# A list scheduler gets ten more rounds with shaken keys: the order of the attention stage in a gated linear attention and mixture-of-experts kernel

## The chip, the cores and the metric

The kernel runs on one core of a Trainium2 chip. The metric is device time in microseconds (us); lower is better. The core has five engines that run side by side, each through its own instructions in their order: TensorE (PE in the profile, its weight loads PEld), VectorE (DVE), ScalarE (ACT), GpSimd (POOL) and SyncE (SP), which here only issues transfers (DMA). An instruction that needs another engine's result waits for it, and everything behind it on its own engine waits too. So the order in which each engine's instructions stand decides how long the engines wait for each other.

## The reference

Two blocks follow each other: a gated linear attention and a mixture of experts with one expert per token. With B = 4, H = 8, S = 768 positions, D = 48 per head, N = 3072 tokens of 384 values, 8 experts with 1024 hidden values:

```python
mag = np.sqrt(a_re * a_re + a_im * a_im)
scale = np.minimum(mag, 0.999) / (mag + 1e-06)
a_re_n, a_im_n = (a_re * scale, a_im * scale)
for t in range(S):
    ar, ai = (a_re_n[:, :, t, :, None], a_im_n[:, :, t, :, None])
    new_re = ar * S_re - ai * S_im
    new_im = ar * S_im + ai * S_re
    kv = np.einsum('bhd,bhe->bhde', k[:, :, t], v[:, :, t])
    S_re, S_im = (new_re + kv, new_im)
    y[:, :, t] = np.einsum('bhd,bhde->bhe', q[:, :, t], S_re)
...
x = np.ascontiguousarray(attn_out.transpose(0, 2, 1, 3)).reshape(B * S, H * D)
...
logits = x @ w_gate
expert_idx = np.argmax(logits, axis=1)
...
for e in range(E):
    mask = expert_idx == e
    xe = x[mask]
    h = np.maximum(xe @ w1[e], 0.0)
    ye = h @ w2[e]
    out[mask] = gate_w[mask, None] * ye
```

`gate_w` is the softmax weight of the chosen expert. The change alters no arithmetic: both kernels compute all of this.

## The kernel before

The attention's recurrence is done in chunks of 128 positions: cumulative products of the complex gates (X), queries multiplied with them and keys divided by them, then products of matrices on TensorE. The expert part follows.

What matters here is that the attention part, the routing and the first two tiles of the first expert aren't emitted in the order in which the code stands. Each piece of work becomes an `Op` with an engine, the time in which it keeps that engine busy, a `late` time after which its result can be used, and what it needs. The times are the author's constants:

```python
        def dve(cols, emit, after=(), free=(), first=5):
            return op("V", cols / 960 + 0.068, cols / 960 + 0.19, emit, after, free, first)

        def act(cols, emit, after=(), free=(), first=5, n=1):
            return op("A", n * 0.08 + cols / 1200, n * 0.08 + cols / 1200 + 0.15, emit, after, free, first)

        def pe(passes, emit, after=(), free=(), first=5):
            return op("T", passes * 0.111, passes * 0.111 + 0.45, emit, after, free, first)

        def dma(late, emit, after=(), free=()):
            return op("S", 0.62, late + 1.0, emit, after, free)
```

`after` holds operations whose result it reads, `free` those that must be done before it may overwrite a buffer. `turns` walks through time: whenever an engine is free, it takes the able operation with the smallest key.

```python
def turns(ops, needs, users, ready, key, begin):
    ...
    for _ in ops:
        t, e = min((max(clock.get(e, 0.0), min(x[0] for x in l)), e) for e, l in able.items() if l)
        x = min((x for x in able[e] if x[0] <= t), key=lambda x: key[x[1]])
        able[e].remove(x)
        clock[e] = begin(x[1], t, clock.get(e, 0.0))
        ...
```

`in_time` does this ten times. The first round's key is the longest way to the end. After each round the schedule is run backward from the end, and the latest starts found there become the keys of the next round. The round whose schedule ends first, by those constants, is kept.

```python
def in_time(ops):
    ...
    key = {o: (o.first, -way[o]) for o in ops}
    best = None
    for _ in range(10):
        start, slow, twice = {}, [0.0], set()
        ...                                   # TensorE counts double for a while after an idle time
        turns(ops, needs, users, lambda o: ..., key, begin)
        end = max(start[o] + o.late for o in ops)
        if best is None or end < best[0]:
            best = end, sorted(ops, key=lambda o: start[o]), start

        back = {}
        ...
        turns(ops, users, needs, lambda o: ..., {o: -start[o] - o.busy for o in ops}, begin_back)
        key = {o: -back[o] - o.busy for o in ops}
    return best[1]
```

At the end the operations are emitted in the kept order: `for o in in_time(ops): o.emit()`. Each engine then runs its own in that order.

The steps of one tile (two and two thirds heads of one batch) that are spoken of below: `fold` sums squares on VectorE (`fs`), takes Ln and Exp on ScalarE (`fl`), corrects that value by a Newton step on VectorE and multiplies queries and keys into packs, which transfers move to `QX` and `KX`, one buffer per head:

```python
                o = dve(n, lambda: vtt(s, f2[:, 0], f2[:, 1], ALU.add), [sq], old["fs"])
            ...
            ln = act(n, lambda: A.activation(l, s2, func=ACT.Ln, bias=w_bias[:, 1:2]), [o], old["fl"])
            ex = act(n, lambda: A.activation(l, l, func=ACT.Exp, scale=-1.0), [ln])
            prod = [dve(n, lambda u=u: vtt(q_to[u], pu[u], by_chunk(qs[:, :, at]), ALU.mult), there + [lq], free[0]) for u in range(2)]
            ...
            o = dve(n, lambda: vtt(s, s2, l, ALU.mult), [ex], [g] + old["fs"])
            ...
            o = dve(n, lambda: vstt(l, s, -2.0, l, ALU.add, ALU.mult), [o])
            o = dve(n, lambda: vtt(l, l, ks[:, :, at], ALU.mult), [o, lk])
            kprod = [dve(n, lambda u=u: vtt(k_to[u], pu[u], by_chunk(l), ALU.mult), [o], free[1]) for u in range(2)]
```

`front` builds the products X; between blocks it carries a state on (`carry`, `zc`), which reads `last`, copied by ScalarE. `attention` runs per chunk and pair of heads: a score matmul from KX and QX into a PSUM bank, a masking product on VectorE (`ak<-bank,causal`), a copy on ScalarE, the output matmuls, their copy `ys`, a transpose of the state, its copy `st` (read by the next chunk's outputs), and a matmul that mixes the heads into rows `xf`. `send` routes finished rows and moves them to `sorted_x`; `early` computes the first two tiles of the first expert. Then come all experts, which are written in plain order and aren't in the list.

## Time and profile before

| | before |
|---|---|
| time, median of 3 runs | 665.49 us (665.45 to 667.85) |
| span of the profiled execution | 662.9 us |
| TensorE busy | 547.0 us (83%), mean granted clock 0.932 |
| VectorE busy | 368.9 us (56%) |
| ScalarE busy | 289.4 us (44%) |
| GpSimd busy | 79.0 us (12%) |
| moved by transfers | 89.81 MB, 135 GB/s |

The shares of the whole span mix two parts. The page also gives the busy time in forty slices of the span, where they come apart, and the trace answers for any stretch. A busy TensorE is not TensorE at its peak, since matmuls are pipelined and their ends are modelled. A wait is put down to the operation that came last before it ended.

### The profile page before, as it was taken

Reading aid. Unit: us, or ns where it says so; the run is one execution under the profiler, and the core shown is the slowest. Engines: PE = TensorE matmul, PEld = TensorE weight load, DVE = VectorE, ACT = ScalarE, POOL = GpSimd, SP = SyncE. Lnnn points to the kernel's source line nnn. Section 1 sums busy time; section 2 is a strip of 40 time slices with the busy share of each in tenths; the row PEclk is TensorE's granted clock in tenths of the full one; section 3 lists DMA queues with packets and bytes.
Section 4 is the critical chain, followed back from the end, with each engine's and each line's share of the span. In section 5 each row is a group of like instructions: output and inputs, shape, how many; then the busy total and the mean of one; then the engine's idle time right before and its main releaser. Section 6 shows DMA issues by size and latency. Waiting matters only on the chain. (4 is left out here: it accounts for less than half of the span.)

```text
span 662.9 us, 8204 instructions
## 1 busy us (share of the span) xinstructions
PE 547.0 (83%) x2594; PEld 334.5 (50%) x2594; DVE 368.9 (56%) x782; ACT 289.4 (44%) x940; POOL 79.0 (12%) x96
## 2 busy tenths in 40 slices
PE   1541288968899478968998999999999999999993
PEld 0220145636565345645566675555555555655552
DVE  5999999999999999999735121111111202010100
ACT  6555488788998788866743101010111100010100
POOL 9100000000004004003003110111101020101111
PEclk9865599998999689988999999999999999999997
DMA  9694866277624766178479434444554440100000
GB/s 260 144 244 118 194 166 160 80 191 174 177 72 130 188 158 177 52 172 203 107 275 400 89 130 124 139 141 138 151 139 135 117 124 32 36 6 24 9 12 29
DMA packets 77635, 89.81 MB, mean 135 GB/s; under 512 B 25341, under 2 KB 67343, under 8 KB 75536
## 3 DMA queue, kind: packets, MB, share of 16 engines
q1 hardware_dynamic: 74000, 79.33, 44.3%
q0 software_dynamic: 3584, 9.87, 4.2%
q8 instruction: 22, 0.36, 0.2%
q14 instruction: 29, 0.24, 0.1%
HBM read 54.31 MB, written 16.63 MB: 107 GB/s over the span
## 5 line engine op out<-in xcount | busy, mean ns | idle before, releaser
L136 PE MATMUL bank<-xt,big 128*128 128x448 f32 (+1 forms) x384 | 136.1, 514 | 1.1 <-DVE xt L888 1.1
L136 PE MATMUL bank<-big,ht 128*128 128x384 f32 (+1 forms) x608 | 136.8, 420 | 0.0
L136 PE MATMUL bank<-QX,KX 128*128 128x224 f32 (+1 forms) x384 | 94.4, 378 | 35.0 <-DMA KX<-pk 26.1
L136 PEld LDWEIGHTS bank<-big,ht 128*128 128x128 f32 (+1 forms) x608 | 84.5, 168 | 53.6 <-issue 7.0
L136 PEld LDWEIGHTS bank<-xt,big 128*128 128x128 f32 x384 | 71.1, 190 | 63.3 <-issue 60.8
L136 PEld LDWEIGHTS bank<-QX,KX 128*128 128x128 f32 x384 | 68.5, 205 | 51.1 <-issue 34.7
L136 ACT ACTIVATE big<-big 128x576 f32<-128x576 f32 (+3 forms) x77 | 68.6, 903 | 16.4 <-DVE big L136 15.1
L909 DVE TENSOR_SCALAR ht<-bank 128x448 f32<-128x448 f32 (+1 forms) x32 | 18.9, 591 | 101.9 <-PE bank L136 101.9
L136 ACT ACTIVATE QX<-diag,KX 96x48 f32<-96x48 f32 x280 | 72.5, 335 | 1.9 <-DMA KX<-pk 1.7
L911 ACT ACTIVATE ht<-bank 128x448 f32<-128x448 f32 (+1 forms) x32 | 16.6, 517 | 121.8 <-PE bank L136 121.8
L136 PE MATMUL two<-big,ident 128*128 128x512 f32 (+1 forms) x112 | 43.2, 542 | 29.8 <-ACT big L136 25.8
L788 POOL DMA_INDIRECT sorted_x<-xf,slot x24 | 29.8, 1242 | 316.0 <-DVE big L136 155.3
L136 PE MATMUL bank<-ak,vb 128*48 128x224 f32 (+1 forms) x384 | 54.1, 365 | 15.2 <-ACT ak L136 12.9
L136 DVE TENSOR_TENSOR big<-big,big 128x576 f32<-128x576 f32 (+3 forms) x86 | 65.0, 766 | 0.9 <-ACT big L136 0.2
L922 ACT ACTIVATE yo<-bank,gt 128x384 f32<-128x384 f32 x15 | 8.7, 581 | 122.4 <-PE bank L136 122.4
L136 DVE TENSOR_TENSOR big<-big 128x288 f32<-128x288 f32 (+5 forms) x108 | 55.2, 518 | 6.2 <-ACT big L136 5.4
L269 POOL DMA_INDIRECT out_dram<-yo,to x22 | 21.4, 972 | 230.1 <-ACT yo L922 184.9
L136 DVE TENSOR_TENSOR ak<-bank,causal 128x256 f32<-128x256 f32 x96 | 39.9, 417 | 15.3 <-PE bank L136 15.0
L136 PEld LDWEIGHTS two<-big,ident 128*128 128x128 f32 x112 | 22.9, 240 | 49.8 <-issue 32.9
L136 PE MATMUL bank<-QX,st 128*48 128x224 f32 (+1 forms) x320 | 43.3, 350 | 0.8 <-ACT st L136 0.8
L136 PE MATMUL bank<-across,ys 128*128 128x104 f32 x192 | 37.7, 287 | 5.3 <-ACT st L136 2.4
L136 ACT ACTIVATE ys<-bank 128x224 f32<-128x224 f32 (+1 forms) x96 | 32.3, 342 | 16.0 <-PE bank L136 15.6
(126 smaller groups left out, 555.5 us busy)
## 6 DMA issues: line engine op xcount, KB each, us to landing
big<-in_moe_w_dram SPq DMA_DIRECT2D x16, 1536.0 KB, 9.1
KX<-pk SPq DMA_DIRECT2D x44, 146.2 KB, 4.3
QX<-pk SPq DMA_DIRECT2D x44, 144.0 KB, 3.5
sorted_x<-xf SPq DMA_DIRECT2D x8, 731.5 KB, 6.2
xq<-sorted_x SPq DMA_DIRECT2D x28, 168.0 KB, 8.6
big<-in_a_re_dram SPq DMA_DIRECT2D x16, 288.0 KB, 4.6
big<-in_a_im_dram SPq DMA_DIRECT2D x16, 288.0 KB, 4.5
qt<-in_q_dram SPq DMA_DIRECT2D x12, 384.0 KB, 3.9
```

The lines of the kernel that those rows point to most:

```text
L136: return lambda *a, **kw: self.tc.keep_in_program_order(f(*a, **kw))
L269: move = nc.gpsimd.indirect_dma_start(out=rows, out_offset=bass.IndirectOffsetOnAxis(ap=index, axis=0), in_=y, in_offset=None, bounds_chec ...
L788: move = nc.gpsimd.indirect_dma_start(out=sorted_x[:, :], out_offset=bass.IndirectOffsetOnAxis(ap=slot[:, i:i + 1], axis=0), in_=xfs[(b * ...
L909: nc.vector.tensor_scalar_max(ht[:, f, cols], h, 0.0)
L911: nc.scalar.activation(ht[:, f, cols], h, func=ACT.Relu)
L922: nc.scalar.activation(y, o, func=ACT.Copy, scale=gt[:, i, 0:1])
```

## The change

The scheduler gets twenty rounds in place of ten. The first ten are as before. From the eleventh on, every key gets a random shift before the round: up to 4 us either way in the eleventh, 0.6 times as much in each further round (2.4, 1.44, ..., 0.04 us). The shifts come from a small generator of numbers with a fixed first value, so that the build always gives the same order. The best round of all twenty is kept, again by the author's constants. The purpose is to leave an order on which the forward and backward passes have settled, and to try others near it.

```diff
+SHAKE = 2004214
 ...
 def in_time(ops):
+    bits = SHAKE * 2862933555777941757 + 3037000493
+
+    def shake(width):
+        nonlocal bits
+        bits = (bits * 6364136223846793005 + 1442695040888963407) % (1 << 64)
+        return ((bits >> 33) / (1 << 30) - 1) * width
+    for _ in range(4):
+        shake(0)
     needs = {o: list(dict.fromkeys(o.after + o.free)) for o in ops}
 ...
     key = {o: (o.first, -way[o]) for o in ops}
     best = None
-    for _ in range(10):
+    for turn in range(20):
+        if turn >= 10:
+            key = {o: key[o] + shake(4 * 0.6 ** (turn - 10)) for o in ops}
         start, slow, twice = {}, [0.0], set()
```

The kept order before comes from the fifth round; the kept order after comes from the seventeenth, the seventh of the new ones.

## The prediction

> **What bounds the kernel now.** I read the views from coarse to fine: the slices of the page, the table of stretches, then the waits and the order in time of VectorE.

> First the slices of the page, each digit a fortieth of the span (16.6 us), in tenths of busy time:

> ```profile
> PE   1541288968899478968998999999999999999993
> DVE  5999999999999999999735121111111202010100
> ACT  6555488788998788866743101010111100010100
> ```

> VectorE stands at 9 from the second slice to the nineteenth, then TensorE at 9 to the end. So there are two regimes, one after the other. I took the seams from the order of instructions in time and asked for the busy time of each stretch. Columns: from and to, length, then busy us and count for PE, PEld, DVE, ACT, POOL, and the granted clock, DMA share and GB/s.

> ```profile
> 6.20:20.00 13.80, 4.50 (x8) 2.27 (x8) 10.35 (x15) 10.58 (x17) 13.13 (x20) 1.00 0.80 228
> 20.00:324.15 304.15, 220.84 (x1294) 141.80 (x1295) 297.05 (x584) 232.78 (x800) 23.97 (x18) 0.87 0.60 156
> 324.15:353.95 29.80, 27.39 (x206) 19.12 (x207) 12.22 (x40) 13.55 (x56) 0.00 (x0) 1.00 0.73 264
> 353.95:379.69 25.74, 23.01 (x98) 15.85 (x97) 7.39 (x45) 4.01 (x17) 6.81 (x7) 1.00 0.68 217
> 379.69:652.95 273.26, 271.22 (x993) 155.42 (x991) 39.04 (x82) 25.85 (x48) 29.31 (x31) 1.00 0.31 90
> ```

> The reader is to see four things. From 20 to 324 us VectorE works 297.05 of 304.15 us: **7.1 us of idle time are all that an order can take from it directly**. From 324 to 380 us TensorE works 50.4 of 55.5 us: first the rest of attention, then the two early tiles of the first expert. From 380 us the experts keep TensorE at 271.2 of 273.3 us. And 10 us of end follow. The experts are not in the list that the change reorders.

> Who holds VectorE in those 304 us is in its waits (total, times, longest):

> ```profile
> DVE fs L136 <- ACT fl L136: 2.2, 3, 1.2
> DVE zc L136 <- ACT last L136: 1.2, 2, 0.7
> DVE big L136 <- ACT big L136: 0.5, 2, 0.4
> DVE free_row L136 <- ACT big L136: 0.2, 1, 0.2
> ```

> That is 4.1 us in 8 waits, all for ScalarE, none for a DMA or a matmul. The other 3.0 us lie in gaps too short to be listed. Six lines of VectorE's order in time (start, busy us) show what these are:

> ```profile
> 316.69 0.55 DVE L136 TENSOR_TENSOR pk<-big,qt 128x384 f32<-128x384 f32 x1
> 317.16 0.41 DVE L136 TENSOR_TENSOR ak<-bank,causal 128x256 f32<-128x256 f32 x1
> ...
> 318.23 0.54 DVE L136 SCALAR_TENSOR_TENSOR fl<-fs,fl 128x384 f32<-128x384 f32 x1
> 318.81 0.56 DVE L136 TENSOR_TENSOR fl<-fl,kt_in 128x384 f32<-128x384 f32 x1
> 319.40 1.03 DVE L136 TENSOR_TENSOR pk<-big,fl 128x384 f32<-128x384 f32 x2
> ...
> 323.34 0.56 DVE L136 TENSOR_TENSOR fs<-fs,fl 128x384 f32<-128x384 f32 x1 [1.22 <-ACT fl L136]
> ```

> Where the next operation doesn't read the one before it, it starts ahead of that one's recorded end: 317.16 against 316.69 + 0.55 = 317.24, so 0.08 early. Where it does read it, it starts after: 318.81 against 318.77, 319.40 against 319.37. Over the whole stretch I took the medians: 67 such pairs at +0.034 us, the other neighbours at -0.082 us. **A dependent pair side by side costs 0.116 us more** than the same two with something else between them. The last line is the longest of the eight waits.

> [...] The trace shows 0.50 in the slice from 60 to 80 us, after a wait of 26.1 us for the first KX; nothing in the change removes that wait, as shown below.

> **The change part by part.** No instruction is added or removed on the chip: the ten extra rounds are work of the build. Both orders hold the same 675 operations on VectorE, 710 on ScalarE, 435 on TensorE, 268 transfers on SyncE and 26 on GpSimd. So busy sums stay, and only waits can change. I compared the two built orders, engine by engine and place by place.

> 1. What stays. VectorE's order is the same for its first 70 operations, TensorE's for its first 5, ScalarE's for its first 45. The start (6 us before the first product, the idle time to 20 us) and the half clock before 80 us therefore stay. The round that won is the seventh of the ten new ones, with 490 of VectorE's 675 operations in other places, by 3 places on average.

> 2. What lies ahead of the end. I added up VectorE's durations from the trace ahead of the last product into KX (the last head's keys): 307.4 us of work in both orders, a difference of 0.0. For the first head of the second batch it is 4.2 us later, for the second tile of the last batch 1.0 us earlier. So the new order puts no less work in front of the critical product; VectorE can reach it sooner only by idling less.

> 3. Dependent pairs. Up to that product the old order has 71 neighbours in which the second reads the first, the new one 58. 13 x 0.116 us = 1.5 us less.

> 4. The eight waits. A product `fs<-fs,fl` waits for Ln and Exp on ScalarE; what hides them is the VectorE work between the sum of squares and that product. Old and new, in us of such work: 2.15 and 4.29 at the product that now waits 0.77 us (at 84.7 us), 2.12 and 3.48 at the one that waits 0.11 (132.2 us), 0.82 and 1.47 at the one that waits 1.22 (the last line above). Of the 13 products nine get more cover, two of them (227.5 and 317.5 us) 0.3 to 0.4 us less, the rest about the same. For `zc<-last,carry`, which waits for two copies on ScalarE: 0.63 and 1.90 at 117.1 us, 1.18 and 1.10 at 199.9 us (waits 0.51 now), 1.26 and 0.65 at 305.5 us (waits 0.67 now), so one may get worse. I count 0.8 + 0.1 + 0.6 us saved and 0.2 us lost, so **4.1 us of named waits become about 2.8**, and 0.2 for smaller ones: 1.5 us less. ScalarE's own queue was moved too, by 6 places on average, and that I can't add up; it makes this term the loosest.

> 5. The tail. TensorE idles 5.1 us between 324 and 380 us, in waits of at most 0.9 us for ScalarE and VectorE on a chain that goes back and forth (outputs, their copy, transpose, its copy, next outputs). The new order keeps that chain; the last chunk's scores stand at places 376 and 377 of 435 in place of 377 and 379. The transfers change more: the last six loads of KX are issued only from 329.4 us now, behind four loads of sorted rows and three of QX, though their products end at 326.5 us. In the new order four QX loads go ahead of the first KX, in time in which SyncE waits anyway. TensorE has other work at that point, so I count 0 for the tail, with 1 us either way.

> Sum: -1.5 - 1.5 + 0 = **-3.0 us**. TensorE idles 2 to 7 us in most stretches of 20 us between 80 and 324 us, so an earlier VectorE should pull it along, and the experts, 273.3 us, follow unchanged. 665.5 - 3.0 = 662.5 us.

> **The rivals.** *VectorE was never the limit that matters; the chain on TensorE is.* For it: from 324 us on TensorE is full, and if its work before that is held by copies on ScalarE (15.2 us in 15 waits for `ak` alone), VectorE's gain ends as a longer wait. Against it: TensorE idles throughout. It would give 665 us. *ScalarE takes over.* It works 19.8 of 20 us from 160 to 180 us and 19.7 in the next 20, so a VectorE that is 3 us ahead there meets a full queue, and operations that the shaking put in front of a needed Exp would cost VectorE new waits. It would give 665 to 668 us. *Transfers.* SyncE issues in one queue, each issue some 0.6 us; one moved behind a late source blocks all behind it. The eleven loads of the tail were reordered, so a loss of 1 to 3 us there is possible: 664 to 667 us.

> **Range and chances.** The dependent pairs are counted, so that term is firm to half a us; the waits may end anywhere from -3 to +2 us; the tail within 1.5 us. Together some 3 us either way: 659.7 to 665.8 us. The 7.1 us of idle time in the first regime and the 5.1 us in the tail cap a gain at 12.2 us, under 2% of 665.5 (13.3 us), so faster by over 2% is nearly out of reach; a loss of that size would need one transfer or wait gone badly wrong.

> **What would show it.** In the changed profile: the stretch from 20 us to the last `fs<-fs,fl` near 321 us in place of 323.3, with VectorE idle near 5 us in it; named waits of VectorE near 2.8 us, still for ScalarE; the first matmul of the experts near 376.7 in place of 379.69 us; the experts at 273 us. Wrong I would be if VectorE's waits rose or named a DMA or a matmul, if its lead were there at 320 us and gone at 377, or if the experts' stretch itself moved.

## The result, and the profile after

The changed kernel takes 672.25 us (median of 4 runs, 670.41 to 672.66) against 666.12 us before in the same session: **ratio 1.0083, 95% interval 1.0054 to 1.0111**, so 0.8% slower. Run once more beside other kernels it took 672.91 us, ratio 1.0101 (1.0076 to 1.0127). The prediction was 662.5 us, at most 665.8: wrong in sign. By the scheduler's own constants the kept order ends 3.6 us earlier than the old one (373.03 against 376.64 us); on the chip it ends 6 to 7 us later. Most single executions of one kernel lie within 3 us of their median, so a ratio counts here only with its interval.

The profiled execution has a span of 668.6 us (662.9 before). First the slices of the page:

```profile
PE   1551278967979587978898999999999999999993
DVE  5999999999999999899934102102111202010110
ACT  6555498877997778767843110010000010010100
```

VectorE's row of nines is broken once, in the slice from 267 to 284 us, and lasts one slice longer than before (the twentieth is a 9). Then the stretches, with seams at the same instructions as before (columns: from and to, length, busy us and count of PE, PEld, DVE, ACT, POOL, then granted clock, DMA share, GB/s):

```profile
20.00:330.82 310.82, 222.25 (x1295) 143.08 (x1295) 296.88 (x583) 233.41 (x800) 23.16 (x18) 0.86 0.61 153
330.82:360.85 30.03, 27.62 (x211) 19.32 (x211) 12.69 (x45) 14.05 (x60) 1.68 (x2) 1.00 0.76 277
360.85:385.35 24.50, 22.72 (x92) 15.31 (x91) 7.51 (x40) 3.59 (x13) 5.12 (x6) 1.00 0.67 208
385.35:658.90 273.55, 271.23 (x993) 155.42 (x991) 39.25 (x82) 25.85 (x48) 29.53 (x31) 1.00 0.31 90
```

The whole loss stands in the first line. It is 6.7 us longer than before (310.82 against 304.15), with the same VectorE work (296.88 against 297.05): VectorE idles 13.9 us instead of 7.1. The tail (30.03 + 24.50 = 54.5 us, against 55.5) is 1.0 us shorter, the experts are 0.3 us longer. The first expert matmul starts at 385.35 us (379.69 before). Who holds VectorE in the first stretch (total, times, longest):

```profile
DVE zc L148 <- ACT last L148: 2.0, 1, 2.0
DVE fs L148 <- ACT fl L148: 1.7, 3, 0.9
DVE free_row L148 <- ACT QX L148: 1.6, 1, 1.6
DVE big L148 <- ACT big L148: 1.6, 3, 1.1
DVE fs L148 <- ACT big L148: 1.4, 1, 1.4
DVE big L148 <- ACT xf L148: 0.8, 1, 0.8
...
```

All lines together are 11.1 us in 15 waits, against 4.1 in 8 before; 9.8 us of them name ScalarE, 1.3 us a matmul. `fs<-fs,fl`, the wait that I had worked on, did shrink (1.7 after 2.2; the 1.22 us before the last product is gone). What is new are single waits of 1 to 2 us at places where the old order had none: for `last`, for a `QX` copy, for products into `big`. The largest is at 273.77 us. This is ScalarE, then TensorE, in order of time just before it (start, busy us; in brackets idle time before, and what ended it):

```profile
264.54 0.68 ACT L148 ACTIVATE big<-big 128x576 f32<-128x576 f32 x1 [1.02 <-issue]
266.44 0.36 ACT L148 ACTIVATE ys<-bank 128x224 f32<-128x224 f32 x1 [1.22 <-remote]
...
269.22 0.27 ACT L148 ACTIVATE st<-bank 96x128 f32<-96x128 f32 x1 [1.76 <-PE bank L148]
...
273.21 0.34 ACT L148 COPY last<-big 128x192 f32<-128x192 f32 x1
273.45 0.29 ACT L148 ACTIVATE last<-big 128x96 f32<-128x96 f32 x1
```

```profile
264.00 0.55 PE L148 MATMUL bank<-QX,st 128*48 128x224 f32 x4
266.85 0.31 PE L148 MATMUL bank<-ident,ys 128*96 128x128 f32 x1 [2.30 <-issue]
```

The copies into `last` wait for nothing themselves: they stand in ScalarE's queue behind `ys` and `st` copies that came late and the QX products behind those. And `ys` at 266.44 us is odd. It reads a matmul whose record ends at 264.55 us, everything else it needs is older, yet it starts 1.9 us after that end and 1.2 us after the engine was free. In a second profile of the same kernel these are 4.1 and 3.45 us. In the profile of the kernel before, no operation that waits for TensorE has such an unexplained gap of over 0.5 us.

### The profile page after: what moved, and what is told of

It is laid out like the page before. It is cut to its first block, busy times and chain, and to the rows that moved or that the text cites. A ratio compares the mean times of both kernels' runs of the same rounds, so it can differ in the third digit from the quotient of the medians.

```text
span 668.6 us, 8184 instructions
## 1 busy us (share of the span) xinstructions
PE 548.3 (82%) x2594; PEld 335.4 (50%) x2594; DVE 369.5 (55%) x782; ACT 290.3 (43%) x940; POOL 78.0 (12%) x96
## 5 line engine op out<-in xcount | busy, mean ns | idle before, releaser
L148 PE MATMUL bank<-QX,KX 128*128 128x224 f32 (+1 forms) x384 | 92.1, 373 | 8.7 <-ACT QX L148 3.6
L148 PE MATMUL two<-big,ident 128*128 128x512 f32 (+1 forms) x112 | 46.9, 578 | 58.1 <-DVE big L148 31.5
L923 ACT ACTIVATE ht<-bank 128x448 f32<-128x448 f32 (+1 forms) x32 | 16.6, 517 | 121.8 <-PE bank L148 121.8
L148 ACT ACTIVATE ys<-bank 128x224 f32<-128x224 f32 (+1 forms) x96 | 32.3, 343 | 19.7 <-PE bank L148 16.7
```

What stands on the lines that cost most here:

```text
L148: return lambda *a, **kw: self.tc.keep_in_program_order(f(*a, **kw))
L923: nc.scalar.activation(ht[:, f, cols], h, func=ACT.Relu)
```

## The experiments

Theories at the start. **Queue**: in ScalarE's queue the new order puts operations that VectorE needs behind others, each place costing a wait of its own. **Transfers**: SyncE's new order is the cause. **Bank**: some operations start only after matmuls into *other columns* of the same PSUM bank (`bank` in the views, where the outputs of matmuls lie), or after reads of such columns, waits that the list of needs doesn't hold (I compared each start with all it waits for: 9.9 us of such waits on ScalarE and 5.5 on TensorE before; 12.9, 5.1 and 1.8 on VectorE after). **Chance**: an end by the constants is no measure at this scale, and the old order is simply a good draw. All ratios are to the kernel before, in the same session.

### Which part of the order

SyncE's queue alone in the old order, the other engines' queues as changed:

```diff
+        old, new = in_time(ops, 10), in_time(ops, 20)
+        queues = {e: [o for o in (old if e == "S" else new) if o.engine == e] for e in "VATPS"}
 ...     # emitted so that each engine keeps its own queue and every need comes first
```

> The changed kernel, but SyncE issues its transfers in the order of the kernel before; the orders of VectorE, ScalarE and TensorE are the changed ones. If ScalarE's in-order queue is the cause (operations that VectorE waits for stand behind others), transfers don't matter: 671 to 673 us, the last fs<-fs,fl again near 331 us and VectorE's named waits near 11 us. If the new order of the transfers is the cause: back to 665 to 667 us.

Measured: 697.63 us, ratio 1.0458 (1.0429 to 1.0486). Both expectations fall. VectorE now waits up to 10.9 us in one piece for ScalarE, and 8.3 us in all for transfers out of the packs. The orders of the queues fit each other, and this mix costs more than either; so the run doesn't tell what the new transfer order costs in its own place.

Then each half of the old order with the other half of the new one:

```diff
-        for o in in_time(ops):
+        old, new = in_time(ops, 10), in_time(ops, 20)
+        head = set(old[:1100])
+        for o in old[:1100] + [o for o in new if o not in head]:
```

> The first 1100 of the 2114 operations (to about 222 us) in the old order, the rest in the new one. If the loss is made of separate waits, each from its own place in the orders, only those after 222 us stay: 3 to 4 us over the kernel before, near 669.5 us, with the step that starts at 218.1 us in the old profile again near 218. If one place early in the order sets everything off, nothing is lost: 665 to 667 us. If the waits are chance meetings of the queues, the later ones need not come back when the queues arrive by another way: anything between 663 and 671 us, with waits at other places than in the changed kernel.

> The other way round: the first 1100 operations in the new order, the rest in the old one. Separate waits: the 3.3 us that the changed kernel has lost at 222 us stay, near 669 us, and the sum of the two losses (this and the other half) is that of the whole change, about 6 us. One early place: all of the loss, near 672 us. Chance meetings: the sum of the two halves is not 6 us.

Measured: old then new 670.31 us, 1.0040 (1.0015 to 1.0065); new then old 668.64 us, 1.0034 (1.0015 to 1.0053). The halves add up to 0.74%, the whole change to 0.83 and 1.01%: within the intervals, as separate waits would. The waits also come with their half. With the new first half VectorE waits 1.6 us for QX at `free_row` as in the changed kernel; with the new second half the late `ys` is back (3.37 us), with a wait for `last` of 1.5 us behind it.

The changed kernel itself, again:

> The changed kernel as it is, once more, beside the others of this batch, because single executions of one kernel lay up to 8 us apart so far. Every theory: 671 to 672.5 us, ratio near 1.008. If it is nearer 669 us, half of the first difference was scatter, and the alternating banks did nothing.

As told above: 672.91 us, 1.0101. The loss is no scatter.

### The waits inside a bank

Such a wait in the kernel before: the copy `st` at 304.55 us reads a transpose whose record ends at 304.31 us (304.04 + 0.27), and starts 0.03 us after the end of the matmuls `bank<-across,ys` (304.15 + 0.37 = 304.52), which write other columns of the same bank.

The four places for the outputs lie two and two in banks 4 and 5, used in turn. The edit makes neighbours in time use different banks; nothing else moves:

```diff
-        yst_ps = [p[:, i * (128 + R2):(i + 1) * (128 + R2)] for p in ps[4:6] for i in range(2)]
+        yst_ps = [p[:, i * (128 + R2):(i + 1) * (128 + R2)] for i in range(2) for p in ps[4:6]]
```

> The changed order, but the four places for the outputs alternate between the two PSUM banks, so that one place's copy and the next place's matmuls are in different banks; the trace shows operations that wait for a matmul or a copy in another part of the same bank, which the list of needs doesn't hold (12.9 us of such waits on ScalarE, 5.1 on TensorE, 1.8 on VectorE in the changed kernel, against 9.9, 5.5 and 0 before). If those waits make the loss, this brings 3 to 6 us: 666 to 669 us. If ScalarE's queue order makes it by itself: within 1.5 us of 672 us.

> The old order with the outputs' places alternating between the two banks. If waits inside one bank are a cost that both orders pay, it gains too: 664 to 665.5 us. If they hurt the new order alone: 666 to 667.5 us, no difference.

Measured: in the new order 669.21 us, 1.0040 (1.0023 to 1.0058), so it takes 0.4 to 0.6% off; in the old order 669.35 us, **1.0059 (1.0044 to 1.0075), so it costs 0.6%**. Neither branch for the old order was right. The same edit helps one order and harms the other by as much, and after it the two orders are level. So where these waits fall can move the time by as much as the whole difference. How much of them is left after the edit was not counted in either order; that they make the loss isn't shown. That the program waits so is in the traces (`st` above, by 0.24 us); whether it has to wasn't tried.

### ScalarE's load

The diagonal products into QX fill ScalarE's queue between the operations that VectorE waits for. In the same place of the same order they go to GpSimd:

```diff
-                        for w in range(2):
-                            A.activation(QX[i][0:R2, c, 128 + w * D:128 + w * D + D], diag[:, w, :], func=ACT.Copy, scale=...)
+                        P.tensor_tensor(out=QX[i][0:R2, c, 128:]..., in0=diag, in1=bc(KX[i]..., [R2, 2, D]), op=ALU.mult)
```

> The changed order, with the same order of all queues, but the diagonal products into QX (which fill ScalarE's queue between the operations that VectorE waits for) are issued on GpSimd, one operation in place of two. If ScalarE's full queue makes the waits: the waits for last, big and fl shrink to some 3 us or less, the last fs<-fs,fl comes at 322 to 325 us in place of 330, time 662 to 667 us. If the order of VectorE and TensorE themselves makes them: 670 to 672 us. Rival: GpSimd is slow at it or gets in VectorE's way, and the scores wait longer: above 672 us, with waits that name GpSimd.

> The same move of the diagonal products to GpSimd in the old order. If a full ScalarE is the cause of the difference between the orders, this gains less than the changed order does (it had 4.1 us of such waits, not 11.1): 663 to 666 us, and the two orders come within 2 us of each other. If GpSimd is in the way: above 668 us, as in the changed order.

Measured: 692.87 us, 1.0398 (1.0367 to 1.0429), and 684.16 us, 1.0263 (1.0234 to 1.0292). The rival held. From the groups of the new order's run (busy, mean ns), and TensorE's and VectorE's waits:

```profile
L148 POOL TENSOR_TENSOR QX<-diag,KX 96x96 f32<-96x96 f32 x140 | 87.6, 658 | 183.3 <-DMA KX<-pk 181.1 <-issue 2.1
```

```profile
PE bank L148 <- POOL QX L148: 15.6, 5, 8.1
```

```profile
DVE ak L148 <- PE bank L148: 4.6, 4, 3.0
...
DVE fs L148 <- ACT fl L148: 2.0, 2, 1.5
```

One product takes 658 ns there (the pair on ScalarE about 490: three in a row take 1.47 us at 269.73 us of the changed kernel), the scores wait for it, and VectorE for the scores. The waits for `last` and QX did vanish, but into longer ones. As a test of the queue theory the pair decides nothing.

### The late results of TensorE

From 261.6 us on, GpSimd starts five indirect row moves in a row (transfers that put finished rows into `sorted_x` at places held in a table), while SyncE moves QX and KX. The stretches from 262 us of the changed kernel (columns as above):

```profile
262.00:266.00 4.00, 2.54 (x19) 1.78 (x19) 3.81 (x8) 1.92 (x8) 3.09 (x4) 1.00 0.96 253
266.00:270.00 4.00, 2.74 (x15) 1.35 (x15) 3.45 (x10) 1.81 (x9) 1.60 (x2) 0.75 0.80 252
```

The DMA engines are busy to 0.96, TensorE to 2.54 of 4 us; then its clock drops. Transfers of instructions aren't in the way: none lies between 258 and 268.7 us, nor in the gap of the second profile. The next run holds the five moves back until VectorE has started a product at 273.9 us:

```diff
+        later = [o for o in order if o.engine == "P"][7:12]    # emitted after that product
+        held.append(...)                                       # the product's name
 ...     # in away():
+                    if held:
+                        tc.add_manual_dep(move, held[0], ..., reason="held")
```

> The changed order, but five of the six indirect row moves that GpSimd starts between 261 and 268 us wait until VectorE has started the product big<-big at 273.9 us; nothing reads or overwrites those rows before 312 us. If the load of the DMA engines there (over 0.9) is what makes TensorE's results late at 264 to 269 us: the late start of the copy ys at 266 to 269 us is gone, VectorE's wait for last at 273.8 us shrinks from 2.0 to below 1 us, and the time falls by 2 to 4 us to 668 to 670.5 us. If the row moves have nothing to do with it: 671.5 to 673 us, the late start still there.

Measured: 668.97 us, 1.0056 (1.0037 to 1.0076). The stretches, then ScalarE in order of time at the same operations:

```profile
262.00:266.00 4.00, 3.59 (x27) 2.36 (x27) 3.23 (x6) 2.71 (x14) 0.00 (x0) 1.00 0.93 194
266.00:270.00 4.00, 2.97 (x20) 2.07 (x21) 3.90 (x12) 3.55 (x16) 0.00 (x0) 1.00 0.63 110
```

```profile
265.77 0.68 ACT L148 ACTIVATE big<-big 128x576 f32<-128x576 f32 x1 [1.01 <-DVE big L148]
266.36 0.34 ACT L148 ACTIVATE ys<-bank 128x224 f32<-128x224 f32 x1
```

`ys` now starts at once behind `big<-big`, no idle time in between, TensorE does 3.59 of 4 us and keeps its clock, and the wait of `zc` for `last` is gone from VectorE's list. So the 2.0 us that the list of waits puts down to ScalarE's `last` had their cause two engines further back. The other waits stay: VectorE's list to 330 us still adds up to 9.4 us. The control, the same hold in the old order:

> A control: the old order with the same five row moves held until VectorE has started the same product (at 268.4 us there; they start at 256.8 to 264.4 us now). The old order has no late results of TensorE there. If the row moves cost only where they make results late: 665 to 666.5 us, as before. If holding them relieves every order: 662 to 664 us, and the changed order's gain from it says nothing of its loss.

Measured: 665.69 us, 1.0001 (0.9988 to 1.0014). Holding the moves is worth nothing where no result was late. What in the moves delays TensorE's results, their own packets or GpSimd's work for them, isn't told apart: the hold removes both. A high share of the DMA engines alone doesn't do it: it is 0.93 in the held run too. Nor do row moves and a high share together suffice, since the kernel before has both here, and no late result:

```profile
258.00:262.00 4.00, 2.62 (x21) 1.25 (x17) 4.00 (x9) 2.45 (x8) 3.63 (x2) 1.00 0.93 254
```

Both helpful edits together:

> The changed order with both edits that helped it alone: the five row moves held (3.9 us) and the outputs' places alternating between the banks (3.7 us). If the two take away different losses: 665 to 667 us, level with the kernel before. If they share one (the late results at 264 to 269 us were much smaller with alternating places already): 668 to 669.5 us.

Measured: 668.56 us, 1.0037 (1.0019 to 1.0054). They share what they take away; some 0.4% stays.

### Orders as draws

If chance decides, orders that look alike to the scheduler must lie apart on the chip. I chose four by what the profiles measured, by a replay, a small calculation: every operation with its median duration from seven profiles, the measured hand-overs, the waits inside a bank, and windows of TensorE's clock, an assumption of mine from what the last section reads in the traces. The edit is only another first value and the round that is kept:

```diff
-SHAKE = 2004214
+SHAKE, TURN = 85, 19
 ...
-        if best is None or end < best[0]:
+        if turn == TURN:
```

> The same scheduler and the same shaking, another first value (85), and its twentieth round is kept. By the scheduler's constants this order ends at 375.24 us, 1.4 us before the old order (376.64) and 2.2 us after the changed one (373.03). I replayed orders with what the profiles measured: each operation's own duration (median of seven profiles), the hand-over from engine to engine (0.03 to 0.07 us), the waits between different columns of one PSUM bank, which the list of needs doesn't hold[...]. The replay puts the changed order 5 us behind the old one, as on the chip, and this one 4.3 us ahead of the old. If the replay holds what decides: 661 to 663.5 us. If the constants were right: 664 to 665.5 us. If an order's time can't be told ahead: 666 to 672 us like the other neighbours.

> First value 457, nineteenth round. By the constants it ends at 375.31 us, as early as the one before it here (375.24) and 1.3 us before the old order. In the replay it ends 12 us after the old order. If the replay's terms (measured durations, waits inside a bank, the clock's windows) decide: 675 to 681 us. If the constants were right: 664 to 666 us.

> First value 368, nineteenth round. By the constants it ends at 377.53 us, 0.9 us after the old order, so the scheduler would drop it. In the replay it ends 3.3 us before the old order. Replay: 661.5 to 664.5 us. Constants: 666.5 to 668 us.

> First value 24, twentieth round: of several hundred first values the one whose kept order ends earliest by the constants (373.88 us, 2.8 us before the old order, nearly as early as the changed one's 373.03). The replay puts it 1.5 us before the old order. Constants and replay nearly agree: 663 to 665 us. If a better end by the constants is worth nothing or less on the chip: 667 to 672 us.

The first and the last of these leave one need out: one load of the next batch's values is issued ahead of one pair of heads' output matmul that reads the old ones (in the list the load waits for the second pair of the last group only). So that product has other values in it; operations and sizes are as in any other order. The three orders below have the need added.

> First value 333, eighteenth round, the outputs' places alternating between the two banks, and one missing need added to the list (the load of the next values of a batch waits for both pairs of heads of the last group, not for the second alone). Out of 8420 orders it is the best but one in the replay with measured durations, bank waits and clock windows, averaged over small random changes of the durations: 4.0 us before the old order. By the constants: 374.12 us, 2.5 us before it. The four orders tried before showed about 0.6 of what the replay promised. Replay: 662.5 to 664.5 us. If the replay is no better than the constants (which have been wrong by 3 to 9 us): 666 to 670 us.

> First value 251, nineteenth round, alternating places and the added need: best in the replay, 4.1 us before the old order; by the constants 375.81 us, only 0.8 us before it. Replay: 662.5 to 664.5 us. Constants: 664.5 to 666 us. Neither: 666 to 670 us.

> First value 361, twentieth round, with the added need and the places as in the kernel before: 2.9 us before the old order in the replay, 2.0 us before it by the constants (374.64). Replay: 663.5 to 665 us. Neither: 666 to 670 us.

| order (first value) | end by the constants | replay against the old order | measured, us | ratio, 95% interval |
|---|---|---|---|---|
| old (none) | 376.64 | 0 | 665.6 to 666.9 | 1 |
| changed (2004214) | 373.03 | +5 | 672.25, 672.91 | 1.0083 and 1.0101 |
| 24 | 373.88 | -1.5 | 668.68 | 1.0039 (1.0023 to 1.0054) |
| 333, alternating places | 374.12 | -4.0 | 663.33 | 0.9962 (0.9950 to 0.9975) |
| 361 | 374.64 | -2.9 | 664.23 | 0.9977 (0.9964 to 0.9989) |
| 85 | 375.24 | -4.3 | 663.97 | 0.9956 (0.9934 to 0.9978) |
| 457 | 375.31 | +12 | 671.40 | 1.0080 (1.0055 to 1.0106) |
| 251, alternating places | 375.81 | -4.1 | 662.46 | 0.9956 (0.9938 to 0.9973) |
| 368 | 377.53 | -3.3 | 664.24 | 0.9974 (0.9955 to 0.9993) |

The two orders with the best ends by the constants are slower than the old one. The order with the worst end is faster. 85 and 457 end 0.07 us apart by the constants and 7.4 us apart on the chip. The replay has the sign right in seven of eight (the changed order's was known when it was made) and mostly promises too much; 24 it has wrong (VectorE waits 5.2 us there for `fl`). It is rough, too: it put 457 12 us behind the old order, where 5 to 6 us were measured. Still, five of the orders that it puts ahead beat both kernels, by 0.2 to 0.4%. Part of that goes with TensorE's clock: over the runs of 85, 333 and 251 its mean is 0.934, against 0.926 to 0.927 for the kernel before beside them. By the slope found there between executions (1.9 to 2.2 us for each 0.01) that is, as an estimate, some 1.5 us of their 2.5 to 3 us. The waits of the best (251):

```profile
DVE ak L148 <- PE bank L148: 2.6, 3, 1.4
DVE big L148 <- ACT big L148: 2.1, 6, 0.6
DVE fs L148 <- ACT fl L148: 1.3, 2, 0.8
DVE zc L148 <- ACT last L148: 0.3, 1, 0.3
```

That is 6.3 us, more than the old order's 4.1. VectorE's idle time in its regime is 8.0 us (7.1 before) and the first expert starts at 379.24 us (379.69): the profiled execution shows hardly a gain, and only the six runs do (661.68 to 664.50 us). For 333 the profile does show it: 6.3 us of idle time, first expert at 376.53 us.

## Why the prediction was wrong, step by step

- **What stays** (1) and **work ahead of the end** (2) held. VectorE's busy sum in its regime is the same to 0.2 us.
- **Dependent pairs** (3) held as counted: after 20 us there are 54 such pairs in place of 67, at +0.034 us again, the other neighbours at -0.082. The 1.5 us don't show in the sum: outside the waits of over 0.15 us, gaps and overlaps between VectorE's neighbours together fell by only 0.3 us, since other small gaps arose.
- **The eight waits** (4) is the step that failed: 4.1 us became 11.1, not 2.8. Of the waits that I followed, those of 1.22 and 0.11 us are gone as worked out and that of 0.77 us became 0.30; but the product whose cover shrank by 0.3 to 0.4 us (227.5 us before) now waits 0.87. The larger part, 7.4 of the 11.1 us, lies at operations that the step did not follow (all but `fs<-fs,fl` and `zc<-last,carry`). I had measured how much VectorE work covers a wait, and not when the operation waited for would be ready; I wrote that ScalarE's queue couldn't be added up and then entered zero for it. What the runs show in its place: the late results behind the row moves (holding these, 1.0083 or 1.0101 became 1.0056) and the places of the outputs in the banks (0.4 to 0.6% in this order), with a common part. That ScalarE's full queue by itself makes the rest was not shown, and some 0.4% isn't traced to a cause. The neighbours of the old order that I tried (halves, other places, the first value 24) lie 0.3 to 0.6% above it as well.
- **The tail** (5) held within its 1 us: 54.5 us in place of 55.5. So part of the loss was made good behind it: 6.7 us at the end of the first stretch, 5.7 at the first expert.
- Of the rivals, "ScalarE takes over" came nearest by its sign (VectorE's waits, nearly all for ScalarE), but its 665 to 668 us were still too low. "Transfers" had a point that I hadn't seen: not SyncE's queue, but GpSimd's row moves. Of what I named as making me wrong, the rise of VectorE's waits came true, and 1.3 us of them name a matmul.
- Behind step 4 is a thought that no step stated: that an order chosen for an earlier end by the constants would at worst do nothing. The table of orders shows ends from 373 to 378 us that say nothing of the sign. The old order may also be a better one than most, since it stood in a kernel already tuned; too few orders were run to show it.

## What to carry to other kernels

Here a list scheduler's predicted gain of 1% was below its own error; its list holds neither the waits inside a PSUM bank nor what transfers do to results, and only a coarse rule for the clock. Run several of its orders and keep by measurement, or price them with measured durations. Follow a wait past the engine that the list names: the cause of the longest one here was two engines back, in transfers that nobody waited for. And when an order changes, add up the queue of the engine that is waited for, not only the cover in front of the wait.
